# Two outputs of each tile pair copied into a tile of another pool, and one small conversion added to the constants

## The chip, the core and the metric

The kernel runs on one core of a Trainium2 chip. Its engines are TensorE (PE, matmuls; PEld is its loading of weights), VectorE (DVE), ScalarE (ACT), GpSimd (POOL) and SyncE (SP), which issues nearly all transfers. Each engine works through its own queue in order, and a wait at the head of a queue holds all that stands behind it. Working memory is SBUF (128 partitions); matmuls write to eight PSUM banks of 128x512 f32. The metric is the time of one execution on the device in microseconds (us); lower is better.

## What is computed

A gated recurrence runs over two sequences of 6080 steps with 256 channels; its result goes through a feed-forward layer of 256 to 2048 to 256 with a piecewise activation. The reference, cut to that:

```python
sig = 1.0 / (1.0 + np.exp(-f_logit))
f = lower_bound + (1.0 - lower_bound) * sig
for t in range(S):
    h = f[:, t] * h + (1.0 - f[:, t]) * x[:, t]
    y[:, t] = h
h = y.reshape(B * S, D) @ w_in
g = np.where(h >= 1, h, np.where(h <= -1, 0.0, (h + 1) ** 2 / 4))
out = g @ w_out
```

## The kernel before

**Tiles.** All data lie with channels on partitions, 256 channels being two halves, k or d = 0 and 1. The 12160 tokens are cut into 24 tiles: the first of 384 tokens, the others of 512. Tiles 0 to 3 are worked off in a start phase of some 175 us, in which the weights are also loaded and split. The other twenty form ten pairs (a, b), a being the earlier tile and b the later.

**Precision.** A matmul of f32 accuracy is made of three with operands split in a high and a low part (`xhi`, `xlo`; `wi_hi`, `wi_lo`; `ghi`, `glo`).

**The steps.** A pair takes eight steps (`NU`), one for each 256 of the 2048 hidden channels; a step's table of times is 10.2 us long (`TG`), and there are 80 steps. Step g makes four 128x512 blocks of hidden values out of seven products instead of eight (Strassen's way, in PSUM banks called Z, Y, Q, V), and adds the output products of step g - 1 (`fill_mm`, line 545) to four accumulators, two for each tile of the pair. Each block goes through a chain: `s_clip` on VectorE (line 934), `s_sq` on ScalarE (941), `s_max` on VectorE (946), the high part on ScalarE (949), the low part on GpSimd (952). Between these, ScalarE copies bank Y to a new bank Q (`fork`, line 914) and bank Z to SBUF (`snap`, 909); TensorE needs the fork before the third product of the step, and VectorE forms Z and V with the help of snap (917, 921).

**The order.** Every engine's queue in this phase follows the list `ev`: each call is entered with a time (`at_time`), the list is sorted by that time, and the code is written out in that order. The times only set the order. The start phase has its order from the string `ORDER` and a planner, `Plan`.

**Pools.** A pool gives out a fixed number of buffers for each tag, and a tile that takes over a buffer waits for all that used its last tenant. Tag `g` (128x2x512 f32, three buffers) holds the activations of two blocks, so each step takes two tiles of it. Tag `o` (128x512 f32, two buffers) holds outputs on their way to memory. Tag `bank` is the eight PSUM banks. Which buffer a tile takes over is settled when the program is built.

**A pair's end.** In the step after a pair's last one, its accumulators are copied to tiles of tag `o` and written to memory by `finish` (lines 575 to 583): b0, b1 and a0 on ScalarE (line 580) at 6.9, 8.5 and 9.2 us of the step, a1 on VectorE (line 582) at 1.9 us of the step after. Nine pairs end so; the tenth ends with `finish_last`.

**Constants.** `lb` is the lower bound, 128x2; the call `constants` makes `oml` = 1 - lb, `mol` = lb - 1 and `omls` from it on VectorE. `mol` is used by `forget`. Ahead of that VectorE sets `one`, and ScalarE computes `warm`, a sigmoid of one element per partition.

Of the kernel before, what the change touches and what calls it, by code (L numbers as in the profile page):

```python
# [7 lines left out]
F32 = mybir.dt.float32  # L8
BF16 = mybir.dt.bfloat16
F32R = mybir.dt.float32r  # L10
I32 = mybir.dt.int32
U32 = mybir.dt.uint32
AF = mybir.ActivationFunctionType
ALU = mybir.AluOpType

P = 128
NMAX = 512
# [131 lines left out]
def gated_scan_then_ffn_kernel(  # L149
# [33 lines left out]
    nc = tc.nc  # L183
    D, NT = outT.shape
    KD = D // P
# [11 lines left out]
    const = ctx.enter_context(tc.tile_pool(name="const", bufs=1))  # L197
# [4 lines left out]
    gp = ctx.enter_context(tc.tile_pool(name="gp", bufs=3))  # L202
    op = ctx.enter_context(tc.tile_pool(name="op", bufs=2))
    pb = ctx.enter_context(tc.tile_pool(name="pb", bufs=8, space=bass.MemoryType.PSUM))

    ov = outT.rearrange("(k p) n -> p k n", p=P)

    lb = const.tile([P, KD], F32, name="lb")
    oml = const.tile([P, KD], F32, name="oml")
    mol = const.tile([P, KD], F32, name="mol")  # L210
# [9 lines left out]
    def bank():  # L220
        return pb.tile([P, NMAX], F32, tag="bank", name="bank")
# [22 lines left out]
    def load_w(j):  # L244
        src, hi, _ = jobs[j]
        raw[j] = sp.tile([*hi.shape, 2], I32, tag="s", name="raw")
        d = raw[j].rearrange("p a b c two -> p (a b c two)" if len(hi.shape) == 4 else "p a b two -> p (a b two)")
        (nc.sync if j else nc.scalar).dma_start(out=d, in_=src.rearrange("(p n) -> p n", p=P).bitcast(I32))
# [323 lines left out]
                    nc.scalar.copy(out=o, in_=p[:, a:b])  # L572
                (nc.sync, nc.scalar)[i].dma_start(out=ov[:, d, s + a : s + b], in_=o)

    def finish(t, d, eng=nc.scalar, dma=nc.sync):
        s, n = tiles[t]
        o = op.tile([P, NMAX], F32, tag="o", name="o")
        p = po.pop((t, d))
        if eng is nc.scalar:
            nc.scalar.copy(out=o[:, :n], in_=p[:, :n])  # L580
        else:
            nc.vector.tensor_copy(out=o[:, :n], in_=p[:, :n])
        dma.dma_start(out=ov[:, d, s : s + n], in_=o[:, :n])

    def bridge(a, b):

# [11 lines left out]

    with tc.manual_schedule():
        nc.vector.memset(one, 1.0)  # L600
        load_w(0)
        nc.scalar.dma_start(out=lb, in_=lower_bound)
        nc.scalar.activation(out=warm, in_=one, func=AF.Sigmoid)
        nc.gpsimd.memset(zero, 0.0)
        po[0, 0] = bank()
        po[0, 1] = bank()
# [21 lines left out]
        def constants(_):  # L628
            nc.vector.tensor_scalar(
                out=oml, in0=lb, scalar1=-1.0, scalar2=1.0, op0=ALU.mult, op1=ALU.add  # L630
            )
            nc.vector.tensor_single_scalar(out=mol, in_=lb, scalar=-1.0, op=ALU.add)
            nc.vector.tensor_single_scalar(out=omls, in_=oml, scalar=2.0**-20, op=ALU.mult)

        def load_f_x(t, k, w):
# [41 lines left out]

        plain = PLAIN.split()
        add("K", "DVE|", 0.25, ["lb"], constants, 0)
        for t in range(NC + 2):  # L680
            z = size(t)
# [22 lines left out]
        for j in range(NJ):  # L704
            z = 0.5 if j < 2 else 1.0
# [22 lines left out]
        for t, u in rest:  # L728
            o = [x for x in order if x not in oorder][0]
# [22 lines left out]
        for kind, t, u, j in pe:  # L752
            z = size(t)
            n = place[t, u]
            i = f"{t}{u}{j}"
            d = 0.0133 + 0.2133 * z
            flat32 = kind + i in plain
            if kind == "H":
                deps = take()
                held.append("T" + i)  # L760
                w = J[j if u == 0 else 1 + 2 * u]
# [17 lines left out]
                if "O" + i not in plain:  # L779
                    deps = ["T" + i]  # L780
                    n = split.index((t, u))
# [8 lines left out]
            else:  # L790
# [7 lines left out]
                w = J[2 + 2 * u]  # L798
# [10 lines left out]
                if u == NU - 1 and j == 1:  # L809
                    for q in range(KD):  # L810
                        add(f"Z{t}{q}", "ACT", act(z), [f"O{i}2{q}"], finish, t, q)
                        if t == T0 - 1:
                            held.append(f"Z{t}{q}")
# [39 lines left out]
        for u in range(NU):  # L853
            w, v = homes[u % 2]
# [13 lines left out]
        def at_time(when, f, *args):  # L868
            ev.append((when, len(ev), f, args))
# [3 lines left out]
        def zt(g):  # L873

            return g * TG
# [106 lines left out]
        def chain(g, z, times):  # L982
            for b, (c, s, m, h, l) in enumerate(times):
                at_time(z + c, s_clip, g, b)
                at_time(z + s, s_sq, g, b)
                at_time(z + m, s_max, g, b)
                at_time(z + h, s_hi_, g, b)
                at_time(z + l, s_lo_, g, b)

        for g in range(NG + 1):  # L990
            z = zt(g)
            last = g == NG
            fills = [1.36, 2.04, 4.08, 4.76, 5.44, 7.48, 8.16, 9.52]
            if last:
                fills = [1.36 + 0.68 * q for q in range(8)]
            for q, w in enumerate(fills):
                if g or q:
                    at_time(z + w, fill_mm, g, q)
            if g and g % NU == 0:
                p = g // NU - 1  # L1000
                a, b = pairs[p]
                if not last:
                    for w, t, d, e in (
                        (6.9, b, 0, nc.scalar), (8.5, b, 1, nc.scalar),
                        (9.2, a, 0, nc.scalar), (TG + 1.9, a, 1, nc.vector),
                    ):
                        at_time(z + w, finish, t, d, e)
                else:
                    at_time(z + TG, finish_last, ((b, 0), (b, 1), (a, 0), (a, 1)))
            if g == 0:  # L1010
                for w, d in ((9.9, 0), (11.3, 1)):
                    at_time(z + w, finish, NC - 1, d)
            if last:
                break
            for q, (w, *product_of) in enumerate(SEVEN):
                if g or q > 2:
                    at_time(z + w, pe1, g, *product_of)
            if g:
                at_time(z + 1.45, fork, g)
                at_time(z + 2.05, snap, g)  # L1020
            at_time(z + 3.9, add_z, g)
            at_time(z + 7.1, add_v, g)
            chain(g, z, (
                (4.6, 5.3, 6.1, 6.8, 7.5),
                (7.8, 8.6, 9.2, 10.0, 10.7),
                (8.5, 9.3, 10.6, 12.85, 13.6),
                (9.9, 10.8, 11.4, 13.5, 15.0),
            ))
# [44 lines left out]
        t, u = NC - 1, NU - 2  # L1073
# [72 lines left out]
```

## Time and profile before

| | us |
|---|---|
| median of 3 runs | 1004.72 |
| lowest and highest run | 1003.25, 1004.91 |
| the profiled execution | 1004.92 |
| its span, from the first to the last instruction | 1003.1 |
| TensorE busy | 993.4 |
| VectorE, ScalarE, GpSimd busy | 742.6, 705.5, 642.3 |

TensorE's granted clock was 0.999 of full speed. A row of the views names an engine, a line of the kernel, the operation, and output and input tiles with buffer numbers left out. "Idle before" is the time that the engine stood still ahead of an instruction, and after an arrow stands what ended it; where several things were awaited it is the one that came last by the profile, and where the one that is named had long been done, it was another. Matmuls overlap: rows give 0.39 us for one of 512 columns, but they start about 0.23 us apart.

### The profile page before, as it was taken

The page shows a single profiled execution, that of the slowest core. Times are in us where ns is not written, and L with a number is a line of the kernel's source. Part 1 is how long each engine was busy: PE and PEld are TensorE (multiplying, and loading weights), DVE is VectorE, ACT ScalarE, POOL GpSimd, SP SyncE. Part 2 cuts the span into 40 slices and gives each one's busy share as a digit, 9 for nine tenths or more (in the row PEclk, how much of TensorE's full clock was granted, in tenths as well). Part 3 has the DMA queues.
Part 4 walks back from the last instruction along what each step waited for, and adds up shares of the span by engine and source line. Part 5 has one row for each costly group of instructions (what it writes and reads, how often), then busy time and mean ns, then how long its engine had stood idle before and what let it go on. Part 6 is the DMA issues. An engine that isn't in the chain of part 4 may idle for free.

```text
span 1003.1 us, 12757 instructions
## 1 busy us (share of the span) xinstructions
PE 993.4 (99%) x4372; PEld 815.8 (81%) x4372; DVE 742.6 (74%) x1128; ACT 705.5 (70%) x1227; POOL 642.3 (64%) x510
## 2 busy tenths in 40 slices
PE   8999999999999999999999999999999999999998
PEld 3788888888888888888888888888888887888886
DVE  7989999776676678677677667667767766776665
ACT  7888898766775775776676677577677667667555
POOL 2132356467767776876877776777687686777454
PEclk9999999999999999999999999999999999999999
DMA  9221030200300120020020020012003002001001
GB/s 345 85 63 64 16 107 1 84 21 1 106 22 1 37 90 1 0 106 22 1 105 22 1 105 22 1 34 93 2 1 105 22 1 84 1 1 43 0 1 43
DMA packets 16913, 46.56 MB, mean 46 GB/s; under 512 B 2000, under 2 KB 3024, under 8 KB 16848
## 3 DMA queue, kind: packets, MB, share of 16 engines
q1 hardware_dynamic: 16416, 45.42, 12.9%
q8 instruction: 34, 0.56, 0.2%
q10 hardware_dynamic: 432, 0.33, 0.1%
q14 instruction: 31, 0.25, 0.1%
HBM read 33.29 MB, written 12.45 MB: 46 GB/s over the span
## 4 chain that ended last, share of the span: by engine, by line
PE 97%; DMA 1%; DVE 1%; ACT 0%; issue 0%; ACTq 0%; DVEq 0%
PE bank L545 51%; PE bank L886 38%; PE bank L455 8%; DMA x<-in_xT 1%; PE bank L474 0%; DMA out_dram<-o 0%; DMA raw<-in_w_in 0%; PE bank L466 0%; DVE h L420 0%; DVE bank L306 0%; ACT g L941 0%; DVE g L511 0%; DVE ea L264 0%; ACT o L580 0%; DVE kept L300 0%
## 5 line engine op out<-in xcount | busy, mean ns | idle before, releaser
L952 POOL TENSOR_TENSOR glo<-g,ghi 128x512 fp32r<-128x512 f32 x320 | 410.8, 1295 | 241.8 <-ACT ghi L949 204.8
L941 ACT ACTIVATE g<-g 128x512 f32<-128x512 f32 x320 | 200.6, 633 | 132.2 <-DVE g L934 129.1
L946 DVE TENSOR_TENSOR g<-g,bank 128x512 f32<-128x512 f32 x320 | 219.5, 686 | 84.7 <-ACT g L941 69.7
L545 PE MATMUL bank<-ghi,wo_hi 128*128 128x512 f32 (+1 forms) x760 | 259.5, 388 | 0.0
L545 PE MATMUL bank<-ghi,wo_lo 128*128 128x512 f32 (+1 forms) x760 | 259.0, 387 | 0.0
L545 PE MATMUL bank<-glo,wo_hi 128*128 128x512 f32 (+1 forms) x760 | 258.9, 387 | 0.0
L949 ACT CAST ghi<-g 128x512 fp32r<-128x512 f32 x320 | 191.4, 625 | 70.3 <-DVE g L946 68.5
L934 DVE TENSOR_SCALAR g<-bank 128x512 f32<-128x512 f32 x320 | 213.7, 689 | 0.4 <-POOL glo L952 0.4
L545 PEld LDWEIGHTS bank<-ghi,wo_hi 128*128 128x128 f32 x760 | 142.5, 188 | 29.3 <-issue 0.5
L545 PEld LDWEIGHTS bank<-glo,wo_hi 128*128 128x128 f32 x760 | 142.5, 188 | 28.7
L545 PEld LDWEIGHTS bank<-ghi,wo_lo 128*128 128x128 f32 x760 | 142.5, 188 | 28.6
L917 DVE TENSOR_TENSOR bank<-bank,snap 128x512 f32<-128x512 f32 x80 | 56.0, 699 | 108.0 <-ACT ghi L949 101.8
L886 PE MATMUL bank<-xhi,s_hi 128*128 128x512 f32 x320 | 124.7, 390 | 1.3 <-ACT bank L914 1.3
L886 PE MATMUL bank<-xhi,s_lo 128*128 128x512 f32 x320 | 124.5, 389 | 0.0
L886 PE MATMUL bank<-xlo,s_hi 128*128 128x512 f32 x320 | 124.5, 389 | 0.0
L886 PE MATMUL bank<-xhi,wi_hi 128*128 128x512 f32 x240 | 93.4, 389 | 0.0
L886 PE MATMUL bank<-xlo,wi_hi 128*128 128x512 f32 x240 | 93.4, 389 | 0.0
L886 PE MATMUL bank<-xhi,wi_lo 128*128 128x512 f32 x240 | 93.4, 389 | 0.0
L529 POOL TENSOR_TENSOR glo<-g,ghi 128x512 fp32r<-128x512 f32 (+1 forms) x31 | 39.0, 1258 | 78.8 <-ACT g L502 18.1
L921 DVE TENSOR_TENSOR bank<-bank,snap 128x512 f32<-128x512 f32 x80 | 56.0, 700 | 42.6 <-PE bank L886 42.6
L914 ACT COPY bank<-bank 128x512 f32<-128x512 f32 x80 | 45.6, 571 | 47.3 <-PE bank L886 47.3
L886 PEld LDWEIGHTS bank<-xhi,s_hi 128*128 128x128 f32 x320 | 60.1, 188 | 14.6 <-ACT bank L914 2.2
(85 smaller groups left out, 1202.2 us busy)
## 6 DMA issues: line engine op xcount, KB each, us to landing
f<-in_fT SPq DMA_DIRECT2D x23, 512.0 KB, 4.2
x<-in_xT SPq DMA_DIRECT2D x23, 512.0 KB, 4.5
out_dram<-o SPq DMA_DIRECT2D x45, 256.0 KB, 2.1
raw<-in_w_out SPq DMA_DIRECT2D x8, 512.0 KB, 4.1
raw<-in_w_in SPq DMA_DIRECT2D x7, 512.0 KB, 5.2
out_dram<-o SPq DMA_DIRECT2D x3, 192.0 KB, 2.0
f<-in_fT SPq DMA_DIRECT2D x2, 192.0 KB, 3.6
x<-in_xT SPq DMA_DIRECT2D x2, 192.0 KB, 4.1
```

Source lines behind the costliest of these rows:

```text
L455: nc.tensor.matmul(out=acc[t, u, j][:, :n], lhsT=(wi_lo if q == 1 else wi_hi)[:, u, k, j], rhs=(xlo if q == 2 else xhi)[t, k][:, :n], star ...
L529: eng.tensor_tensor(out=glo[t, u][:, s, :n], in0=gg[t, u][:, s, :n], in1=ghi[t, u][:, s, :n], op=ALU.subtract,)
L545: nc.tensor.matmul(out=po[t, d][:, :n], lhsT=w, rhs=b if q == 2 else a, start=not begun, stop=(last and q == 2),)
L886: nc.tensor.matmul(out=dst, lhsT=w, rhs=r, start=(start and q == 0), stop=(q == 2), skip_group_check=True,)
L914: nc.scalar.copy(out=B[g, "Q"], in_=B[g, "Y"])
L917: nc.vector.tensor_tensor(out=B[g, "Z"], in0=B[g, "Y"], in1=snaps[g], op=ALU.add)
L921: nc.vector.tensor_tensor(out=B[g, "V"], in0=B[g, "Y"], in1=snaps[g], op=ALU.add)
L934: nc.vector.tensor_scalar(out=gtile(gG, g, b, F32, "g"), in0=B[g, blocks[b][0]], scalar1=-1.0, scalar2=1.0, op0=ALU.max, op1=ALU.min,)
L941: nc.scalar.activation(out=c, in_=c, func=AF.Square, bias=0.5, scale=0.5)
L946: nc.vector.tensor_tensor(out=c, in0=c, in1=h, op=ALU.max)
L949: nc.scalar.copy(out=gtile(hG, g, b, F32R, "ghi"), in_=gtile(gG, g, b, F32, "g"))
L952: nc.gpsimd.tensor_tensor(out=gtile(lG, g, b, F32R, "glo"), in0=gtile(gG, g, b, F32, "g"), in1=gtile(hG, g, b, F32R, "ghi"), op=ALU.subtract,)
```

## The change

`finish` gets a flag, `wide`, that is set for the later tile of a pair. With it, both outputs b0 and b1 go to the two halves of one tile of tag `g`, which is taken when b0 is copied; the copies, their engines, their lines of the table and their transfers stay. a0 and a1 still take tiles of tag `o`. The parameter `dma` was never used with another value and goes.

Two small tiles join the constants. `far` is set to -9 x 2^30 on VectorE; ScalarE converts it to int32 in `edge`, below the range of that type, so that the lowest int32 is to come out, whose bits read as f32 are -0.0. `mol` is now lb - 1 plus these bits, in a form with two tensor operands.

```diff
-    def finish(t, d, eng=nc.scalar, dma=nc.sync):
+    wide_o = {}
+
+    def finish(t, d, eng=nc.scalar, wide=False):
         s, n = tiles[t]
-        o = op.tile([P, NMAX], F32, tag="o", name="o")
+        if wide:
+            if t not in wide_o:
+                wide_o[t] = gp.tile([P, 2, NMAX], F32, tag="g", name="o")
+            o = wide_o[t][:, d]
+        else:
+            o = op.tile([P, NMAX], F32, tag="o", name="o")
         p = po.pop((t, d))
...
-        dma.dma_start(out=ov[:, d, s : s + n], in_=o[:, :n])
+        nc.sync.dma_start(out=ov[:, d, s : s + n], in_=o[:, :n])
...
         nc.vector.memset(one, 1.0)
+        far = const.tile([P, KD], F32, name="far")
+        edge = const.tile([P, KD], I32, name="edge")
+        nc.vector.memset(far, -9.0 * 2.0**30)
         load_w(0)
         nc.scalar.dma_start(out=lb, in_=lower_bound)
         nc.scalar.activation(out=warm, in_=one, func=AF.Sigmoid)
+        nc.scalar.activation(out=edge, in_=far, func=AF.Identity, scale=1.0)
...
-            nc.vector.tensor_single_scalar(out=mol, in_=lb, scalar=-1.0, op=ALU.add)
+            nc.vector.scalar_tensor_tensor(
+                out=mol, in0=lb, scalar=-1.0, in1=edge.bitcast(F32), op0=ALU.add, op1=ALU.add
+            )
...
-                        at_time(z + w, finish, t, d, e)
+                        at_time(z + w, finish, t, d, e, t == b)
```

Apart from the two new instructions ahead of the first gate, the instructions stand in the same order on every engine. What moves is which buffer a tile takes, and with it the waits. Below are ScalarE's instructions at the first pair's end, before. A number behind a name is the buffer's; the brackets name the semaphores waited for, DMAHW with a number being one of the transfers' eight.

```order
L580 COPY o_2505<-bank_1870 128x512 [waits DMAHW0_49,PE_49]
L580 COPY o_2519<-bank_1871 128x512 [waits DMAHW3_49,PE_49]
L941 ACTIVATE g_2487<-g_2487 128x512 [waits DVE_49]
L580 COPY o_2528<-bank_1845 128x512 [waits DMAHW6_49,PE_49,Activation_49]
L941 ACTIVATE g_2522<-g_2522 128x512 [waits DVE_49]
L949 CAST ghi_2503<-g_2487 128x512 [waits DVE_49]
L941 ACTIVATE g_2522<-g_2522 128x512 [waits DVE_49]
L914 COPY bank_2562<-bank_2545 128x512 [waits PE_49,Activation_49]
```

The same place on ScalarE in the changed kernel (o_2509 is the tile of tag g, o_2531 is a0's):

```order
L587 COPY o_2509<-bank_1874 128x512 [waits PE_49]
L587 COPY o_2509<-bank_1875 128x512 [waits PE_49]
L954 ACTIVATE g_2491<-g_2491 128x512 [waits DVE_49]
L587 COPY o_2531<-bank_1849 128x512 [waits DMAHW0_49,PE_49]
L954 ACTIVATE g_2525<-g_2525 128x512 [waits DVE_49]
L962 CAST ghi_2507<-g_2491 128x512 [waits DVE_49]
L954 ACTIVATE g_2525<-g_2525 128x512 [waits DVE_49]
L927 COPY bank_2565<-bank_2548 128x512 [waits PE_49]
```

The third copy, a0's, waited for DMAHW6, the transfer of b0; now it waits for DMAHW0, the transfer of the pair before. The first two copies wait for no transfer any more.

VectorE's instructions behind that, from a1's copy on, before:

```order
L582 COPY o_2564<-bank_1846 128x512 [waits DMAHW5_49,DMAHW7_49,DMAHW3_49,PE_49]
L917 TENSOR_TENSOR bank_2538<-bank_2545,snap_2567 128x512 [waits PE_49,Activation_49]
L934 TENSOR_SCALAR g_2590<-bank_2562 128x512 [waits PE_49,Pool_49]
L946 TENSOR_TENSOR g_2590<-g_2590,bank_2562 128x512 [waits Activation_49]
L921 TENSOR_TENSOR bank_2607<-bank_2545,snap_2567 128x512 [waits DVE_49,PE_49]
```

The same place on VectorE in the changed kernel:

```order
L589 COPY o_2567<-bank_1850 128x512 [waits DMAHW5_49,DMAHW3_49,PE_49]
L930 TENSOR_TENSOR bank_2541<-bank_2548,snap_2570 128x512 [waits PE_49,Activation_49]
L947 TENSOR_SCALAR g_2593<-bank_2565 128x512 [waits DMAHW7_49,DMAHW6_49,PE_49]
L959 TENSOR_TENSOR g_2593<-g_2593,bank_2565 128x512 [waits Activation_49]
L934 TENSOR_TENSOR bank_2610<-bank_2548,snap_2570 128x512 [waits DVE_49,PE_49]
```

The waits for DMAHW6 and DMAHW7, the transfers of b0 and b1, now stand at the first clip of the next step (the third row of each).

TensorE's first output matmuls of the new pair, before:

```order
L545 MATMUL bank_2554<-ghi_2503,wo_hi_88 128x512 [waits Activation_49]
L545 MATMUL bank_2555<-ghi_2503,wo_hi_88 128x512 [waits DVE_49]
L545 MATMUL bank_2554<-ghi_2503,wo_lo_89 128x512
L545 MATMUL bank_2555<-ghi_2503,wo_lo_89 128x512
L545 MATMUL bank_2554<-glo_2513,wo_hi_88 128x512 [waits Pool_49]
```

The same place on TensorE in the changed kernel:

```order
L545 MATMUL bank_2557<-ghi_2507,wo_hi_88 128x512 [waits Activation_49]
L545 MATMUL bank_2558<-ghi_2507,wo_hi_88 128x512 [waits Activation_49]
L545 MATMUL bank_2557<-ghi_2507,wo_lo_89 128x512
L545 MATMUL bank_2558<-ghi_2507,wo_lo_89 128x512
L545 MATMUL bank_2557<-glo_2517,wo_hi_88 128x512 [waits Pool_49]
```

The second matmul waited for VectorE, which had emptied its bank; now the bank is the one that ScalarE empties with a0's copy.

## Rows read from the trace of the kernel before

**Rows 1.** The page: busy us, share of the span, instructions of TensorE.
```profile
PE 993.4 (99%) x4372; PEld 815.8 (81%) x4372; DVE 742.6 (74%) x1128; ACT 705.5 (70%) x1227; POOL 642.3 (64%) x510
```
**Rows 2.** Waits of weight loads, 180 to 990 us: total us, times, longest.
```profile
PEld bank L886 <- ACT bank L914: 2.2, 3, 1.7
```
**Rows 3.** The chain in order of time: start us, us, what.
```profile
179.55 2.04 PE bank L545 x9
...
261.15 2.04 PE bank L545 x9
271.46 2.04 PE bank L545 x9
...
832.51 2.04 PE bank L545 x9
...
844.32 2.06 PE bank L545 x9
...
987.14 2.04 PE bank L545 x9
```
**Rows 4.** Timelines at three pair ends: start us, us, instruction, idle before.
```profile
267.11 0.59 ACT L580 COPY o<-bank 128x512 f32<-128x512 f32 x1 [0.72 <-DMA out_dram<-o]
...
430.38 0.59 ACT L580 COPY o<-bank 128x512 f32<-128x512 f32 x1 [0.69 <-DMA out_dram<-o]
...
835.87 5.05 SPq L583 DMA_DIRECT2D out_dram<-o  x3
...
839.98 0.59 ACT L580 COPY o<-bank 128x512 f32<-128x512 f32 x1 [2.23 <-DMA out_dram<-o]
...
842.67 0.50 PE L886 MATMUL bank<-xhi,s_hi 128*128 128x512 f32 x1 [1.32 <-ACT bank L914]
```
**Rows 5.** ScalarE's output copies: durations in ns, idle before (us, times), landings.
```profile
L580 ACT COPY o<-bank x35: 464/587/601, 132.5 to 921.2; 128x512 f32<-128x512 f32 x33, 128x384 f32<-128x384 f32 x2
...
  DMA out_dram<-o: 3.6, 3
  PE bank L886: 1.4, 6
...
DMA to landing us min/median/max: 1.9/2.1/5.1
```
**Rows 6.** Timeline at the first pair's end: tenants of tag g.
```profile
260.19 2.55 POOL L952 TENSOR_TENSOR glo<-g,ghi 128x512 fp32r<-128x512 f32 x2 [0.44 <-POOL xlo L432]
...
265.27 0.59 ACT L580 COPY o<-bank 128x512 f32<-128x512 f32 x1 [0.79 <-PE bank L545]
...
271.56 0.69 DVE L934 TENSOR_SCALAR g<-bank 128x512 f32<-128x512 f32 x1
```
**Rows 7.** Timeline at the second pair's end: a0's copy, the new pair's first matmuls.
```profile
348.33 0.59 ACT L580 COPY o<-bank 128x512 f32<-128x512 f32 x1 [0.24 <-PE bank L886]
...
350.17 0.62 PE L545 MATMUL bank<-ghi,wo_hi 128*128 128x512 f32 x2
```
**Rows 8.** Timeline of the first 11 us: work beside the constants.
```profile
0.80 0.06 DVE L600 MEMSET one<- 128x1 f32 x1 [0.80 <-PEq L1136]
...
2.95 0.20 ACT L603 ACTIVATE warm<-one 128x1 f32<-128x1 f32 x1
...
4.20 0.52 ACT L381 ACTIVATE f<-f 128x384 f32<-128x384 f32 x1 [1.05 <-DMA f<-in_fT]
...
4.47 0.29 DVE L264 TENSOR_SCALAR ea<-raw 128x256 int32<-128x256 int32 x1 [3.60 <-DMA raw<-in_w_in]
...
5.29 0.16 DVE L632 TENSOR_SCALAR mol<-lb 128x2 f32<-128x2 f32 x1
...
6.61 0.61 DVE L316 SCALAR_TENSOR_TENSOR kept<-kept,omls,bank 128x128 f32<-128x128 f32 x2
...
10.62 0.69 DVE L403 TENSOR_TENSOR x<-f,x 128x512 f32<-128x512 f32 x1 [0.27 <-DMA x<-in_xT]
```
**Rows 9.** The page's DMA queues: packets, MB, share of 16 engines.
```profile
q8 instruction: 34, 0.56, 0.2%
```

## The prediction

> **What bounds the kernel now.** I read the page first: TensorE is busy 993.4 us, 99% of the span [rows 1]. So only what makes TensorE stand still, or adds work to it, can move the time. The change adds no matmul and moves none. The next view is therefore the list of waits of TensorE over the steady part, from 180 to 990 us: its weight loads have one row there, three waits for the copy of line 914, which I call the fork [rows 2]. No other engine, pool or DMA held TensorE in those 810 us.
>
> What the three waits cost is read from the chain in order of time. Once per step of the loop (10.2 us by the kernel's own table) a block of nine output matmuls stands in it as one piece. From its first occurrence to its last, 179.55 to 987.14, are 79 steps; 79 x 10.2 is 805.80, and 807.59 passed: 1.79 us were lost [rows 3]. Two of the places can be seen directly: 261.15 to 271.46 is 10.31 (0.11 lost) and 832.51 to 844.32 is 11.81 (1.61 lost). The remaining 0.07 is left for the third wait. The three waits follow pairs' ends, where the four outputs are copied out of PSUM.
>
> Why the fork is late there is seen in the timeline of the worst place [rows 4]. The outputs go in the order b0, b1, a0, a1 (b is the pair's later tile, a the earlier, 0 and 1 the halves of the model width). Tag o has two buffers, so a0 takes the buffer of b0 and its copy waits until b0 has been written to memory. The transfers were issued from 835.87 on. ScalarE stood still for 2.23 us until 839.98, and behind a0's copy in its queue stand two squares, a cast and the fork. TensorE began the matmul that needs the fork at 842.67, after an idle 1.32 us. Two other pair ends show the same wait, of 0.72 us at 267.11 and of 0.69 at 430.38 [rows 4].
>
> The line of the copies says that this happens at every pair's end: idle time before them is put down three times to the output's DMA (3.6 us) and six times to a matmul of line 886 (1.4 us, 0.24 us each) [rows 5]. The six are DMA waits too: a0's copy does not depend on line 886 at all, and a landing after the median 2.1 us [rows 5] is what the gap between b0's copy and a0's copy asks for. So ScalarE waits at all nine pair ends: 0.24 us six times, and 0.72, 0.69 and 2.23 us.
>
> Setting waits against losses gives a rule: 0.72 lost 0.11, 0.69 lost 0.07, 2.23 lost 1.61, 0.24 lost nothing. Each loss is the wait less some 0.62 us. The kernel has 0.62 us of play at a pair's end, and only slow landings use it up. Landings go from 1.9 to 5.1 us [rows 5].
>
> **The change part by part.** *b0 and b1 go to a tile of g's pool.* The copies themselves are unchanged, 587 ns in the middle on ScalarE [rows 5], and so are their transfers. What goes is the wait: a0 now takes a buffer of tag o that was last used at the previous pair's end, some 82 us earlier, and a1 (on VectorE) takes the other. With the wait gone, the fork stands at its usual place at every pair's end, and TensorE's three losses go with it: 0.11 + 0.07 + 1.61 = 1.79 us. What is late next there? In the six undisturbed pair ends nothing held TensorE, and those already ran with 0.24 us of waiting, so nothing stands just behind. Term: -1.79 us; its bounds are 0 (an execution with no late landing) and -1.79.
>
> *g's pool has one more tenant per pair.* Three tiles of tag g turn over, two per step. At a pair's end the spare one is taken by the outputs, and two tiles of g are taken in an order other than before. The first of these, for the blocks clipped from about 265.2 on, takes a tile whose last readers are the GpSimd subtractions that ended by 262.74 [rows 6]: 2.4 us to spare. The second is the first g tile of the next step and takes the outputs' tile once they are in memory: b1's copy ended at 265.86, the clip that overwrites the tile began at 271.56 [rows 6], so 5.70 us lie between; the median landing leaves 3.6 us, the longest one seen 0.6 us. Term: 0.
>
> *TensorE's banks.* The build hands out the eight PSUM banks in another order from there on. The new pair's second accumulator now lies in the bank that a0's copy has to empty (before: one emptied by VectorE). At an undisturbed pair's end a0's copy ended at 348.92 and the first matmul into that accumulator, the second of two matmuls that start 0.23 apart from 350.17 on, ran at 350.40 [rows 7]: 1.48 us to spare, 1.7 us without the 0.24 of waiting. In the row of 839.98 it would have been half a microsecond too late, but that copy waited for the DMA that is gone. Term: 0.
>
> *The constants.* One memset of 128x2 on VectorE, one conversion of 128x2 on ScalarE, and the operation on mol gets a second tensor. The memset (the one beside it takes 0.06 us) lies in VectorE's 3.60 us before its first real work; the conversion (0.20 us as the warm-up, the nearest row) lies in ScalarE's 1.05 us before the first gate, which waits for its own data until 4.20; without that cover it would cost 0.20 [rows 8]. A second load of a function table would cost more, but the build has one load, as before. The operation on mol took 0.16 us as a one-tensor form; the nearest two-tensor row is 128x128 and takes 0.31 each, two in 0.61 us. So it grows by 0 to 0.15 us; I take 0.02, since two columns are nearer to 0.16 than 128 are. VectorE's next wait for a transfer, 0.27 us before 10.62, absorbs either [rows 8]. Term: 0, with a bound of +0.15.
>
> **The sum.** The profiled execution took 1004.92 us (span 1003.1, so 1.8 us lie around it). 1004.92 - 1.79 = 1003.13. The runs shown have the median 1004.72, 0.20 below it, and go from 1003.25 to 1004.91. The lowest lies 1.67 us below the profiled one, nearly the 1.79 that is at stake: I read it as a run in which no landing was late, and the others as runs with one. The forecast is **1003.1**, which is 0.16% below the median.
>
> What held the transfer no view of this trace shows. The page lists instruction fetches in its table of DMA queues, 34 on one queue of together 0.56 MB, or 16 KB each [rows 9]. On such fetches the Trainium skill (Runtime: NRT & Kernel Launch, section Instruction fetch mechanics) says that instructions are streamed in blocks of 16 KiB by DMA, which the sizes here agree with, and that crossing a block's border is mostly hidden. By that word the late landing would be an accident of this one execution and the first rival's time would come; by the rows a landing of 5.1 us did happen and did stop TensorE.
>
> **The rivals.** *Hidden anyway.* Late landings are rare, the median run has none, and its distance from the lowest run is something that the change leaves alone (the head of the program, or around the span). Then the time stays where it is, **1004.7**. For it: six of nine pair ends lose nothing. Against it: an execution with 1.79 us of losses lasted only 0.20 longer than the median, so the median run must lose about as much.
>
> *A new wait, slower.* The next step's first clip on VectorE now waits for the transfers of b0 and b1. It decides from a landing of 5.7 us on, and what is queued behind it on VectorE is the max, the sum of line 921 and two clips that feed the next step's output matmuls. To end more than 2 us above the median TensorE would have to lose 2.0 + 1.6 = 3.6 us: one landing of over 9.3 us, or 0.4 us at each of nine pair ends. That gives **1006.8**. Against it: the longest landing here is 5.1 us.
>
> *It does not take the wait away.* If b0's and b1's tile or a0's buffer still waited for something near, ScalarE would stand where it stands now: 1004.9. The build's order speaks against it: a0's copy waits for its matmuls and for one DMA, that of the pair before. I count it with the first rival.
>
> *More than forecast.* If every run of before holds such a loss and the lowest is low for another reason, the median falls by 1.79 to 1002.9, or by one more loss of 1.61 to 1001.3; halfway is **1002.1**.
>
> **How the numbers follow.** Forecast 0.74, hidden anyway 0.14, slower 0.06, more than forecast 0.06. What a measurement of this kernel can tell from no change is about 0.2%, 2.0 us, that is below 1002.7 or above 1006.7. Of the forecast's 0.74 some 0.05 lie below 1002.7 through the spread of runs. So faster 0.11, slower 0.07 (0.01 of it for the constants and the unknown), same 0.82. The range reaches from 1002.4, inside the case of more, to 1004.9, which takes in the case of no gain.
>
> **What would show it.** In the changed kernel's profile ScalarE's copies of outputs have no idle time ended by a DMA, and none by line 886; TensorE's weight loads have no wait for the fork between 180 and 990; the 79 steps take 805.8 us; the span is 1001.3; the first gate starts at 4.2 as before. Wrong would be: a landing over 3 us at a pair's end and still a wait before a0's copy; a wait of the clip for an output's DMA; or no waits at all and still a time near 1004.7, which would put the spread of runs somewhere that this trace does not show.

## The result and the profile after

The changed kernel takes **1009.09 us** (median of 4 runs, 1008.92 to 1009.26), against 1003.99 for the kernel before in the same comparison (4 runs, 1002.97 to 1004.91): a ratio of 1.0051, 95% interval 1.0040 to 1.0063. It is slower by half a per cent, where 1003.1 was forecast and 1004.9 was the upper end of the range. Its profiled execution took 1009.26, its span is 1007.4, and the granted clock was 0.999 of full speed as before.

The page of the changed kernel, busy us by engine, against [rows 1]:

```profile
PE 999.2 (99%) x4372; PEld 816.2 (81%) x4372; DVE 742.9 (74%) x1129; ACT 705.9 (70%) x1228; POOL 645.1 (64%) x510
```

TensorE has as many matmuls as before, 4372, and is busy for 5.8 us longer. Its time not busy fell from 1003.1 - 993.4 = 9.7 to 1007.4 - 999.2 = 8.2 us. So it waits less and works longer on the same matmuls. From 180 to 990 us neither its matmuls nor its weight loads have a single row in the list of waits; the fork's row [rows 2] is gone.

The changed kernel's chain in order of time (start us, us, what), against [rows 3]: the block of nine output matmuls once per step.

```profile
179.79 2.06 PE bank L545 x9
190.06 2.06 PE bank L545 x9
...
261.98 2.06 PE bank L545 x9
272.25 2.06 PE bank L545 x9
...
837.28 2.06 PE bank L545 x9
847.56 2.06 PE bank L545 x9
...
991.38 2.06 PE bank L545 x9
```

The 79 steps take 991.38 - 179.79 = 811.59 us, which is 10.273 each, and they are equal: 10.27 from 261.98 to 272.25 and 10.28 from 837.28 to 847.56, the two pair ends that took 10.31 and 11.81 before. The blocks themselves take 2.06 where most of those of before took 2.04. So the losses at pair ends went as forecast, and each step became 0.073 us longer, pair end or not.

ScalarE's copies of outputs in the changed kernel, against [rows 5] (idle before them in us, times, and what ended it):

```profile
L587 ACT COPY o<-bank x35: 465/580/601, 132.2 to 924.6; 128x512 f32<-128x512 f32 x33, 128x384 f32<-128x384 f32 x2
...
  PE bank L545: 7.3, 9
```

The rows for the output's DMA and for line 886 are gone. What is left is one wait per pair end for the accumulator that is to be copied, 0.81 us each; the 0.79 in [rows 6] is such a wait. The landings are as late as before:

```profile
L590 SPq DMA_DIRECT2D out_dram<-o x44: 332/343/884, 132.7 to 928.1; - x44
...
DMA to landing us min/median/max: 1.9/2.1/5.1
```

The 5.1 us belong in both executions to an output that is issued at 187 us, at the end of the start phase. Of the outputs at the pairs' ends the latest landed after 4.2 us in both. One of the changed kernel compares directly with the worst place of before: b0's transfer issued at 429.70 landed after 3.97 us, that of 835.87 before after 4.01. The latter cost TensorE 1.61 us; for the former nothing waited, and its step is 10.27 us like all others.

The changed kernel's first 11 us in the timeline, against [rows 8]:

```profile
0.84 0.06 DVE L610 MEMSET far<- 128x2 f32 x1
...
3.06 0.19 ACT L614 ACTIVATE edge<-far 128x2 int32<-128x2 f32 x1
...
4.19 0.52 ACT L381 ACTIVATE f<-f 128x384 f32<-128x384 f32 x1 [0.94 <-DMA f<-in_fT]
...
5.24 0.15 DVE L643 SCALAR_TENSOR_TENSOR mol<-lb,edge 128x2 f32<-128x2 f32 x1
...
10.58 0.69 DVE L403 TENSOR_TENSOR x<-f,x 128x512 f32<-128x512 f32 x1 [0.23 <-DMA x<-in_xT]
```

The conversion ended before the first gate's data came; the gate still idled 0.94 us ahead of it and started at 4.19. The operation on `mol` takes 0.15 us, 0.01 less than with one tensor. The new instructions cost nothing, as forecast.

Where the time is, then: the span of before 1003.1, less 1.79 at the pair ends, plus 79 x 0.0733 = 5.79 in the steps, plus 0.24 and 0.06 in the start phase and behind the last block (179.55 became 179.79; 1003.1 - 987.14 = 15.96 became 16.02), is 1007.4. What the 0.24 are is not shown: below, the same instructions without the shift of addresses start the first block at 179.43 (e4), and the shift without these instructions at 179.50 (e3).

Which matmuls became longer is told by the view by lines and shapes, TensorE, 180 to 990 us (busy us, mean ns of one, idle before). First three rows of the kernel before:

```profile
L545 PE MATMUL bank<-ghi,wo_lo 128*128 128x512 f32 x635 | 221.2, 389 | 0.0
...
L886 PE MATMUL bank<-xhi,s_lo 128*128 128x512 f32 x318 | 123.7, 389 | 0.0
...
L886 PE MATMUL bank<-xhi,wi_lo 128*128 128x512 f32 x237 | 92.2, 389 | 0.0
```

The same three in the changed kernel:

```profile
L545 PE MATMUL bank<-ghi,wo_lo 128*128 128x512 f32 x632 | 222.1, 392 | 0.0
...
L899 PE MATMUL bank<-xhi,s_lo 128*128 128x512 f32 x315 | 122.5, 389 | 0.0
...
L899 PE MATMUL bank<-xhi,wi_lo 128*128 128x512 f32 x236 | 93.0, 394 | 0.0
```

Matmuls with `wo` and `wi` are longer by 3 to 5 ns, those with `s` (sums of weights, made once in the start phase by eight casts and eight subtractions that start between 143.7 and 173.8 us, and read by TensorE alone from then on) are not. As matmuls overlap, the distance between their starts says more. Of six matmuls with `s` and the six with `wo` behind them, these are the first of each and the first with `wi` that follows. Before:

```profile
201.83 0.39 PE L886 MATMUL bank<-xhi,s_hi 128*128 128x512 f32 x1
...
203.19 0.39 PE L545 MATMUL bank<-ghi,wo_hi 128*128 128x512 f32 x1
...
204.55 0.39 PE L886 MATMUL bank<-xhi,wi_hi 128*128 128x512 f32 x1
```

After:

```profile
202.24 0.39 PE L899 MATMUL bank<-xhi,s_hi 128*128 128x512 f32 x1
...
203.59 0.39 PE L545 MATMUL bank<-ghi,wo_hi 128*128 128x512 f32 x1
...
204.97 0.39 PE L899 MATMUL bank<-xhi,wi_hi 128*128 128x512 f32 x1
```

Six with `wo` took 1.36 us and take 1.38; six with `s` took 1.36 and take 1.35. Averaged over the steps of the trace: before, matmuls start 226.67 ns apart, 680.0 for three in a row, which I call a triple. After, three with `wo` or `wi` take 229.2, 231.7 and 225.8 ns in turn, 686.7 together, and those with `s` still 226.7. A step has 15 such triples, 8 with `wo`, 3 with `wi`, 4 with `s`; 11 x 6.67 = 73.3 ns, which is the whole growth of a step. It is the same in every step, whichever buffers are in use.

`far` and `edge` are 8 bytes wide and take 32 bytes each in a partition, behind the weights in the pool of constants. That moves all that comes later by 64 bytes: the sums `s`, the inputs, `xhi`, `xlo`, `ghi`, `glo`, the outputs. In the build of before all that TensorE reads in the steps begins 64 bytes past a multiple of 256. In the changed kernel `wi` and `wo` still do, and `s` and the activations begin at 128. The triples that became slower are those whose two operands no longer agree.

### The profile page after: what moved, and what is told of

Its sections match the earlier page's. It is cut to its first block, busy times and chain, and to the rows that moved or that the text cites. A ratio compares the mean times of both kernels' runs of the same rounds, so it can differ in the third digit from the quotient of the medians.

```text
span 1007.4 us, 12750 instructions
## 1 busy us (share of the span) xinstructions
PE 999.2 (99%) x4372; PEld 816.2 (81%) x4372; DVE 742.9 (74%) x1129; ACT 705.9 (70%) x1228; POOL 645.1 (64%) x510
## 4 chain that ended last, share of the span: by engine, by line
PE 98%; DMA 1%; DVE 1%; issue 0%; ACT 0%; DVEq 0%; ACTq 0%
PE bank L545 51%; PE bank L899 38%; PE bank L455 8%; DMA x<-in_xT 1%; PE bank L474 0%; DMA raw<-in_w_in 0%; PE bank L466 0%; DVE h L420 0%; DVE bank L306 0%; DVE g L511 0%; DVE ea L264 0%; DVE kept L300 0%; DVE x L403 0%; DVE kept L321 0%; DVE kept L291 0%
```

## The experiments

In all of them the step length is (last block - first block) / 79 from the chain in order of time, and time and change are told separately.

**e1_wide_only: the outputs' tile alone.** The changed kernel without `far`, `edge` and the new form of `mol`:

```diff
-        far = const.tile([P, KD], F32, name="far")
-        edge = const.tile([P, KD], I32, name="edge")
-        nc.vector.memset(far, -9.0 * 2.0**30)
...
-        nc.scalar.activation(out=edge, in_=far, func=AF.Identity, scale=1.0)
```

> The outputs b0 and b1 go to a tile of tag g, without the new constants; every buffer keeps the address that it has before. Theory A (the 64 bytes that the two constant tiles take push the activations to other addresses, and the output matmuls and the a-products of TensorE then start further apart): the step of the loop is 10.20 us as before, no wait of TensorE for the fork, so span 1001.3 and time 1003.1. Theory B (the other turn-over of tag g or of the PSUM banks slows TensorE): step 10.27, time 1009.

Measured: 1002.92 (10 runs, 1002.77 to 1003.16), the kernel before beside it 1004.65 (19 runs, 1002.96 to 1007.04); ratio 0.9988 (0.9978 to 0.9997). The chain of e1:

```profile
179.56 2.04 PE bank L545 x9
189.76 2.04 PE bank L545 x9
...
985.36 2.04 PE bank L545 x9
```

805.80 us, 79 steps of 10.200, no loss at any pair end, and a span of 1001.4. The outputs' tile does what it was forecast to do, and it is not what makes the changed kernel slow.

**e2_constants_only: the constants alone.** Outputs as before:

```diff
-                        at_time(z + w, finish, t, d, e, t == b)
+                        at_time(z + w, finish, t, d, e)
```

> The constants far and edge and the two-tensor form of mol alone; outputs go where they went before. Theory A: step 10.27 us as in the changed kernel, so 5.9 us more than the kernel before, and the waits of a0's copy are back: time 1009 to 1011. Theory B: step 10.20, time 1003 to 1005.

Measured: 1010.16 (4 runs, 1009.39 to 1010.91), ratio 1.0055 (1.0040 to 1.0070). Its 79 steps take 813.03 us, 1.44 more than the 811.59 of the changed kernel; the fork's waits are back, in the list of waits of weight loads from 180 to 990 us of e2 (us, times, longest):

```profile
PEld bank L899 <- ACT bank L927: 1.6, 2, 1.4
```

The slowness is in the constants.

**e3_pad64: 64 bytes and no conversion.** The kernel before, with a tile of 64 bytes that nobody reads:

```diff
         nc.vector.memset(one, 1.0)
+        pad = const.tile([P, 16], F32, name="pad")
+        nc.vector.memset(pad, 0.0)
```

> The kernel before with one more constant tile of 64 bytes per partition behind the weights, set to zero by one memset on VectorE; no conversion, mol as before. Theory A: the same as with the constants alone, step 10.27 us, 1009 to 1011. Theory C (the conversion or the bits that mol gets slow something later): step 10.20, 1003 to 1005.

Measured: 1009.23 (4 runs, 1009.19 to 1010.04), ratio 1.0048 (1.0033 to 1.0063). The chain of e3:

```profile
179.50 2.06 PE bank L545 x9
189.78 2.06 PE bank L545 x9
...
992.20 2.06 PE bank L545 x9
```

The blocks take 2.06 as in the changed kernel, and the 79 steps 812.70, which is its 811.59 and 1.11 lost at pair ends. Neither the conversion to int32 nor the operation on `mol` has a part in it: the bytes do it.

**e4_far_before_weights: the whole change, the two small tiles ahead of the weights.** Now weights and activations move together:

```diff
+    far = const.tile([P, KD], F32, name="far")
+    edge = const.tile([P, KD], I32, name="edge")
     wi_hi = const.tile([P, NU, KD, 2, P], F32R, name="wi_hi")
```

> The changed kernel with far and edge laid ahead of the weights, so that the weights move by the same 64 bytes as the activations. Theory A in its relative form (what counts is how weights and activations lie to each other): step 10.20 us, time 1003.1. Theory A in its absolute form (activations that begin at a multiple of 128 bytes are read slower): step 10.27 or, if weights count too, longer; time 1009 or more. Theories B and C: 1009.

Measured: 1002.96 (10 runs, 1002.83 to 1003.08), ratio 0.9983 (0.9973 to 0.9992). The chain of e4:

```profile
179.43 2.04 PE bank L547 x9
189.63 2.04 PE bank L547 x9
...
985.23 2.04 PE bank L547 x9
```

Steps of 10.200 again, with every instruction of the change in place. What counts is where activations begin relative to the weights, not where they begin.

**How many bytes.** e1 with a pad behind the weights, of 32, 128, 256, 448 and 512 bytes (8, 32, 64, 112 and 128 in the place of `N`; of the three largest only the first 64 bytes are set):

```diff
+        pad = const.tile([P, N], F32, name="pad")
+        nc.vector.memset(pad, 0.0)
```

> The wide outputs without the new constants, and a pad tile of 32 bytes behind the weights: activations begin 96 bytes into a span of 128, weights still 64 into one. Theory H (it counts whether weights and activations begin in the same half of 128 bytes): step 10.20 us, time 1002.9. Theory D (any distance that is not a multiple of 128 bytes costs): step 10.27, time 1008.8, or a step between.

> The same with a pad of 128 bytes: the distance between weights and activations grows by 128. Theories H and D with a period of 128 bytes: step 10.20 us, time 1002.9. If the period is longer (256 bytes or more) or the distance of before was a lucky one: step above 10.20, up to 10.27, time up to 1008.8.

> The wide outputs without the new constants, and a pad of 512 bytes behind the weights. Every tile that TensorE reads again begins at the same place within 512 bytes (320), as before, and 512 bytes further from the weights. Theory P (what counts is the place of weights and of activations within 512 bytes, against each other): step 10.20 us, time 1002.9. Theory L (the distance of before was a lucky one, and any shift costs): step 10.27 to 10.46, time 1009 to 1026.

> The same with a pad of 256 bytes. If the period is 256 bytes or a part of it: step 10.20 us, 1002.9. Theory P with a period of 512: above 10.20; between 10.27 and 10.46 as with the other shifts, time 1009 to 1026.

> The wide outputs without the new constants, and a pad of 448 bytes: the activations lie 64 bytes ahead of the weights' place within 512 bytes instead of 64 behind it. Theory P: step above 10.20 us; if only the size of the difference counted, 10.27 as in the changed kernel and time 1008.8; if its sign counts, another value up to 10.46.

Measured: with 32 bytes 1023.7, step 10.427; with 128 bytes 1026.49, step 10.460; with 448 bytes 1026.41, step 10.460 (one run each; the kernel before 1003.15 beside the first two). With 256 bytes 1002.9 (one run), step 10.200; with 512 bytes 1003.09 (10 runs, 1002.75 to 1005.40), the kernel before 1003.43 beside them (19 runs, 1002.87 to 1005.16), ratio 0.9993 (0.9983 to 1.0003), step 10.200. The chains of the pads of 128 bytes (first three rows) and of 256:

```profile
182.14 2.09 PE bank L545 x9
192.60 2.09 PE bank L545 x9
...
1008.48 2.09 PE bank L545 x9
```

```profile
179.30 2.04 PE bank L545 x9
189.50 2.04 PE bank L545 x9
...
985.10 2.04 PE bank L545 x9
```

So the cost does not grow with the bytes: 256 and 512 cost nothing, 448 (192 past 256) costs as much as 128. Of the distances tried, those that are multiples of 256 are free. The expectation for 32 bytes missed: half the distance cost more than three times as much per step. The one for 128 missed as well, since it put the step at 10.27 at most, and those with a period of 128 bytes are refuted by it.

**Whose bytes.** e1 with pads of their own at other places in the order of pools. e12: 64 bytes ahead of the pool of inputs and 448 behind it, so that the tiles of VectorE and ScalarE alone move (`f`, `x`, `h`), and TensorE's operands by 512:

```diff
+    padp = ctx.enter_context(tc.tile_pool(name="padp", bufs=1))
     ld = ctx.enter_context(tc.tile_pool(name="ld", bufs=2))
     at = ctx.enter_context(tc.tile_pool(name="at", bufs=2))
+    padq = ctx.enter_context(tc.tile_pool(name="padq", bufs=1))
```

> The wide outputs without the new constants; a 64-byte pad ahead of the pools of f, x and h and one of 448 bytes behind them, so that only tiles move within their 512 bytes that VectorE, ScalarE, GpSimd and the DMAs use, while all that TensorE reads in the loop keeps its place there. Theory P: step 10.20 us, time 1002.9. Theory E (TensorE is slowed by other engines' accesses to shifted tiles): step above 10.20, time 1005 to 1026.

Measured: 1002.95 (10 runs, 1002.77 to 1003.05), ratio 0.9990 (0.9981 to 1.0000), step 10.200. The place of `f`, `x` and `h`, which other engines read and write, doesn't matter.

e8: 64 bytes ahead of the pool of g, so that only `wo` and its activations disagree. e9: 64 ahead of the pool of `s` and 64 behind, so that `s` disagrees with `xhi` and `xlo` by 64, `wo` and `wi` with theirs by 128.

> The wide outputs without the new constants, and a 64-byte pad ahead of the pool of g, ghi and glo alone: only the output matmuls read an activation that lies otherwise to its weights. Of a step's 15 triples of matmuls, 11 use the constant weights, so a triple costs 73.3 / 11 = 6.67 ns more in the changed kernel. Theory A relative: 8 triples x 6.67 = 53 ns, step 10.253 us, time 1002.9 + 80 x 0.053 = 1007.2. If another engine's reads of shifted tiles slow TensorE and not its own operands: 10.27 or 10.20.

> The wide outputs without the new constants, a 64-byte pad ahead of the pool that holds the sums of weights s_hi and s_lo, and another behind it: only these weights lie otherwise (activations move by 128). Theory A relative with a period of 128: the four triples with these weights are slower and the eleven others not, 4 x 6.67 = 27 ns, step 10.227 us, time 1005.0. If what counts is the activations' own address: step 10.20, time 1002.9.

Measured: 1020.1, step 10.400, and 1024.82, step 10.440 (one run each); both expectations missed by far. In e8 the view by lines and shapes, 180 to 990 us, shows where the time went:

```profile
L546 PE MATMUL bank<-ghi,wo_hi 128*128 128x512 f32 x624 | 220.7, 394 | 0.0
...
L896 PE MATMUL bank<-xhi,s_hi 128*128 128x512 f32 x311 | 123.8, 398 | 0.0
```

Matmuls with `s` have operands that agree there, and at 398 ns they are longer than those that disagree. A sum over the triples that disagree doesn't hold for all layouts.

e14: 64 bytes ahead of the pool of `xhi`, so that all activations disagree with all weights. e15: 64 ahead of the pool of `s` and 192 behind, so that `s` alone disagrees.

> The wide outputs without the new constants, and a 64-byte pad ahead of the pools of xhi, xlo, g, ghi and glo: every activation that TensorE reads lies 64 bytes further within 256 than every weight, the sums s_hi and s_lo included. Theory W (the weights of a matmul against its own activations): all 15 triples of the step cost what 11 cost in the changed kernel, 15 x 6.67 = 100 ns, step 10.300 us, time 1002.9 + 80 x 0.100 = 1010.9. Theory S (TensorE carries something over, so that a mismatch also slows later matmuls whose own operands agree): without the four agreeing triples that set it back, more than that, 10.35 to 10.46, time 1015 to 1024.

> The wide outputs without the new constants, a 64-byte pad ahead of the pool of s_hi and s_lo and one of 192 behind it: only these weights differ from everything else within 256 bytes. Theory W: four triples cost 6.67 ns more each, step 10.227 us, time 1005.0, and the matmuls of the other eleven triples start 226.67 ns apart. Theory S: the triples behind them start further apart too, step up to 10.46, time up to 1024.

Measured: e14 1011.51, step 10.300; e15 1013.87, step 10.333 (one run each, the kernel before 1004.7). The chains of e14 (first two rows) and of e15:

```profile
179.91 2.06 PE bank L546 x9
...
993.61 2.06 PE bank L546 x9
```

```profile
179.68 2.04 PE bank L547 x9
...
996.01 2.04 PE bank L547 x9
```

In e14 the sum holds: 15 triples x 6.67 = 100 ns on 10.200, and the start times show 229.2, 231.7 and 225.8 in every triple. In e15 four triples at that price would give 10.227, but the price was measured at a distance of 64 bytes, and here it is 192. The first matmuls of two triples with `s`, of the two with `wo` behind them, of one with `wi` and of the next:

```profile
202.22 0.40 PE L899 MATMUL bank<-xhi,s_hi 128*128 128x512 f32 x1
...
203.62 0.39 PE L547 MATMUL bank<-ghi,wo_hi 128*128 128x512 f32 x1
...
205.01 0.39 PE L899 MATMUL bank<-xhi,wi_hi 128*128 128x512 f32 x1
...
205.69 0.39 PE L547 MATMUL bank<-ghi,wo_hi 128*128 128x512 f32 x1
```

The two with `s` take 1.40 us where 1.36 is the undisturbed time, and the two with `wo` 1.39, though their operands agree; the one with `wi` is back at 0.68. Averaged over the steps from 185 to 262 us, a triple with `s` takes 702 ns, or 696 as the second of two in a row; the one or two triples behind take 692 to 697; after that 680 is reached again without another triple with `s`. So four of the eleven triples that agree are slow, and a disagreement can slow later matmuls too.

Is it another engine's work that disturbs? In all runs the tiles `g`, the outputs and snap moved together with `ghi` and `glo`, so the layouts alone don't tell these apart. Two things speak against it. In e15 only `s` stands apart, which no other engine touches in the steps. And at the end of e8's execution the last twelve output matmuls start 233.3 ns apart, against 231.1 on the average of its steps, in this stretch:

```profile
1010.94 0.40 PE L546 MATMUL bank<-ghi,wo_hi 128*128 128x512 f32 x1
1011.02 1.29 POOL L962 TENSOR_TENSOR glo<-g,ghi 128x512 fp32r<-128x512 f32 x1
...
1013.50 0.39 PE L546 MATMUL bank<-glo,wo_hi 128*128 128x512 f32 x1
```

The subtraction on GpSimd is the last work on the activations; beside and behind it VectorE and ScalarE only copy finished accumulators, and the pace of TensorE does not change.

All layouts together, as the distance in bytes (mod 256) between activations and the weights that they meet:

| kernels | `wo` | `wi` | `s` | step, us |
|---|---|---|---|---|
| before, e1, e4, e10, e11, e12 | 0 | 0 | 0 | 10.200 |
| after, e2, e3 | 64 | 64 | 0 | 10.273 |
| e14 | 64 | 64 | 64 | 10.300 |
| e15 | 0 | 0 | 192 | 10.333 |
| e8 | 64 | 0 | 0 | 10.400 |
| e5 | 32 | 32 | 0 | 10.427 |
| e9 | 128 | 128 | 64 | 10.440 |
| e7 | 128 | 128 | 0 | 10.460 |
| e13 | 192 | 192 | 0 | 10.460 |

## Why the prediction was wrong

**What bounds the kernel: right, but one sentence too short.** That TensorE is the bound held. From "adds no matmul and moves none" the prediction went straight to the waits. It took for granted that a matmul of a given shape has a given pace, and never asked whether an operand's place enters it.

**The outputs' tile: right.** The term was -1.79, and e1 shows it: no wait for the fork, 79 steps in 805.80, a span of 1001.4 where 1001.3 was forecast, and a median of 1002.92 where the sum gave 1003.13. The reading of the spread fits the runs: the kernel before ran from 1002.87 to 1007.04 in the 38 runs beside e1 and e12, while e1, e4 and e12 stayed within 0.4 us, 1002.77 to 1003.16. (One run of e10 took 1005.40: its first block starts at 181.80, some 2.4 us late, so it lost that in the start phase, which the outputs' tile doesn't touch.) In those two comparisons the medians differ by 1.73 and by 0.48, so what the tile gives depends on which runs of before are compared. That late landings make the spread is shown where there are traces: in e2 and e3, whose outputs go where they went before, 1.44 and 1.11 us are lost at pairs' ends with a wait for the fork, and in e1, e4 and the changed kernel nothing. Of the runs without a trace it is inferred.

**g's pool and the banks: right.** In the changed kernel the first clip of the next step and the first output matmuls wait for no transfer and no copy; all steps are equal. What the prediction called the slower rival did not occur: landings at the pairs' ends reached 4.2 us, not 9.3. Here one reading of the prediction was wrong: the landing of 5.1 us lies at 187 us and stopped nobody; the one that stopped TensorE took 4.01 (issued at 835.87). It enters no term of the sum. Likewise the fetches are 16 KB each only on the queue that the prediction names; the page's other queue of instructions has 31 of together 0.25 MB, 8 KB each.

**The constants: this is the step that failed.** The term was 0 with a bound of +0.15, worked out from the durations of three instructions and what hides them. All of that held. What was left out is that the two tiles need room: 64 bytes behind the weights moved every later buffer, and a step went from 10.200 to 10.273. The term measures 79 x 0.073 = 5.8 us, and 6.1 with the start phase and the end. e2 and e3 have it without the outputs' tile, e3 without the conversion, and e4 is rid of it with all the instructions kept.

**The rivals.** None named it. The rival on the slower side was put on a wait of VectorE; at 1006.8 it was nearer to the result, but for another reason. The last of the signs given, no waits and yet a time that is too long, is what came, only that the time was not in the spread of runs but in the pace of matmuls.

Could it have been seen? Not in the order of the instructions or in their waits, which are as forecast. The build's addresses show the shift of 64 bytes, but no row of the kernel before tells that it costs anything, since there all operands agree. It would have been a bound to ask for: 45 matmuls a step and 79 steps make 1 ns per matmul 3.6 us.

## What to carry to other kernels

When a kernel is bound by TensorE and a change adds, removes or resizes any tile, however small, compare the addresses that the build gives to TensorE's operands before and after, and look at the distance between the starts of matmuls ahead of any search for waits. Here, put small tiles ahead of the weights (e4, 1002.96), or fill up to 256 bytes (a pad of 256 alone, e11, was free in its one run): the whole change without its shift takes 0.9983 of the kernel before (0.9973 to 0.9992), and no version measured is faster by more than 0.1 us. A busy time that grows at an equal number of instructions is the sign to look for on the page.

## What the runs showed of the hardware

A matmul of 128x128 by 128x512 (fp32r operands) starts 226.67 ns after the one before where all weights and activations of the step begin at the same place within 256 bytes of a partition. Where they did not, intervals from 224 to 241 ns were seen and steps were 0.7 to 2.5% longer; in e7, e8, e13 and e15 matmuls whose own operands agree were slowed with the others. A stop of TensorE disturbs the pace too: in the kernel before, where everything agrees, the matmuls behind the late forks at 270 and 433 us start 229 to 236 and 231 to 232 ns apart, four and two of them, before 226.67 returns. The granted clock was full throughout, between 0.998 and 1.

What inside TensorE does this is not shown. The traces show a weight load of 0.19 us beside each matmul; that weights for the next matmul and activations for the present one disturb each other is a guess that suits a dependence on the distance of the two; no run tests it. Open too is why 64 bytes cost less than 32, 128 and 192, why `wo` alone (e8) costs more than all three (e14), and what held the transfers that landed after 4 us and more.
